# A gated linear recurrence fused with a two-layer MLP: a fourth pair of blocks with two tokens per partition, v reordered by matmul, and a recalibrated instruction order

## The chip, the cores and the metric

The kernel runs on one core of one Trainium2 chip. The metric is the device time of one execution in microseconds (us), lower is better. Of the kernel before there are 11 timed runs, and one execution was recorded by the hardware profiler.

## The reference

For 4 batches, 8 heads, 768 tokens and 48 features per head, a state of 48 x 48 is carried along the tokens, and its output feeds an MLP whose activation is a scaled square of relu plus a bias:

```python
for t in range(S):
    state = alpha[:, :, t, :, None] * state + np.einsum('bhd,bhe->bhde', k[:, :, t], v[:, :, t])
    y[:, :, t] = np.einsum('bhd,bhde->bhe', q[:, :, t], state)
x = y.transpose(0, 2, 1, 3).reshape(3072, 384)
h = x @ w_in                       # 384 -> 2048
r = np.maximum(h, 0.0)
g = s * (r * r) + b
out = g @ w_out                    # 2048 -> 384
```

All inputs and the output are float32; the kernel multiplies in bf16.

## The kernel before

**Blocks.** The 3072 tokens are cut into 24 blocks of 128 (six per batch). Inside a block the recurrence becomes matrix products: the logarithms of alpha are summed along the tokens by a matmul with a triangle of ones (`cum`), exponentials of these sums and of their negatives scale q and k (`qb`, `kb`), scaled q and k are transposed (`T`), their product (`A`, L587) is masked to the triangle (`st_mask`, L597) and multiplied with v (`st_y`, L622); what earlier blocks left comes in through the state (L614), which is updated from k and v (`KV`, `t1`, `snew`). The block's y leaves PSUM (`yevac`), is transposed (`yT`) and lies in `xd` as the MLP's input.

**Two layouts.** The first NPM = 3 pairs of blocks (blocks 0 to 5) are loaded with two neighbouring tokens per partition, so that a contiguous piece of an input is 96 floats (384 bytes); each of the four inputs of a pair is one DMA (L339). From block 6 on, blocks are loaded one by one, one token per partition, with pieces of 48 floats (192 bytes, L346). Four slots per input hold two blocks each (NIN = 4), so a load for block n waits until block n - 8 has been read. In a pair, the tokens of its two blocks lie in the two halves of the partitions, and v must be reordered for `st_y`: it is cast by POOL (L476), half is copied in place (`st_vkeep`, on DVE for pairs 0 and 1, by DMA on SP's queue for pair 2), and half crosses the partitions by DMA (`st_vcross`, from ACT's queue for pairs 0 and 1, from SP's for pair 2). Scaled q and k are transposed by PE up to block 11 and by DMA transposes from SP's queue from block 12 (`st1_Tdma`, L695); y is transposed by PE up to block 13 and by DMA from block 14 (L735).

**The MLP.** Blocks are gathered in groups (GROUPS: 1, 1, 2, 1, 1, 2, 4, 2, 2, 4, 4 blocks). The first product is cut in 96 units of 512 output columns (`mm1`, L755): 12 matmuls of 128 columns, 6 of 256 or 3 of 512, by the size of the group. ACT takes the relu (L764, two buffers `r`), DVE squares it into `gt` (L776). The second product goes in 96 quads (`mm2`, L783), four matmuls of 384 columns each, four quads to a block. The first 12 outputs are scaled by ACT (`oscale`, L815) and get their bias on POOL (`obias`, L824), the later 12 take both steps on DVE (`oevac`, L792). SP stores them. The bias row is made from column sums of w_out (seven large additions on DVE, one float32 matmul, L402).

**Weights.** w_in comes in four quarters by DMAs from POOL's queue, which cast to bf16 on the way (L360). A small copy on POOL (`touch`, L357) ahead of each quarter makes it wait for an input: AFTER = q1, q1, k1, v1. Unit j of a group of one block needs quarter j. w_out comes in four float32 parts by SP's queue and is cast in halves by ACT (L374).

**What sets the order.** A planner in the kernel (`Schedule`) takes a list of operations, each with an engine, an assumed duration, a due time, its tiles and its PSUM bank; it plays the engines forward and always starts the ready operation with the earliest due time. The instructions are emitted in the order of the planned starts, and each engine works its own list in that order. Due times are `want(n)` for block n (from LEAD, UNIT and SHRINK) plus an offset per kind of operation (OFF), and the unit's or quad's number times UNIT for the MLP. SP's loads follow the list LOADS where it names them, then the order of the blocks; moves and stores on SP come as soon as they are ready. Up to 36 us of planned time, small matmuls on zeros (`warm`, L1021) fill planned gaps on PE.

**PSUM.** A of any block goes to one tile of two banks (`a_ps`); the other six banks are handed out by the planner. At most three hold units of the first product.

Of the kernel before, what the change touches and what calls it, by code (L numbers as in the profile page):

```python
# [13 lines left out]
GROUPS = [1, 1, 2, 1, 1, 2, 4, 2, 2, 4, 4]  # L14
LEAD = 28.0
UNIT = 1.7
RING = 8
NPM = 3
NIN = 4
# [5 lines left out]
N_DVE_K = 2  # L25
N_ACT_V = 0
N_ACT_T = 1
N_ACT_X = 2
AFTER = ['q1', 'q1', 'k1', 'v1']
N_POOL_BIAS = 12  # L30
NOUT = 4
TLAT = 3.0
OFF = {'ln': -0.1, 'v': 0.2, 'vk': 0.3, 'vx': 3.95, 'cum': 2.1, 'bl': 1.05, 'ble': 0.2, 'exp': -1.9, 'qb': 0.6, 'kb': 0.1, 'T': -1.6, 'Tc': 0.4, 'KV': 2.65, 't1': 1.2, 'sn': 0.4, 'A': 0.5, 'mask': -1.6, 'y': 1.0, 'ye': 1.2, 'yT': 0.75, 'yTc': 2.9}

LOADS = 'a0 k0 q0 v0 a1 q1 k1 v1 a2 k2 v2 a3 k4 k3 v4 q2 o0 o1 v3 q3 a4 o2 q4 o3 a5 q5 v5 a6 k5 q6 k6 v6 a7 q7 k7 v7 v8 q8 a9 q9 k9 v9 k8 a8 a10 q10 v10 k10'


class Schedule:
# [6 lines left out]
    HOP = 0.3  # L45
    BACKLOG = 4.0

    warm_mates = "cPyYb"
# [11 lines left out]
    def op(self, eng, dur, prio, fn, *args, r=(), w=(), lat=0.1, dma=None, take=(), drop=None):  # L60
        me = len(self.ops)
        deps = set()
# [16 lines left out]
    def run(self):  # L79
# [10 lines left out]
        for i, o in enumerate(self.ops):  # L90
            free.setdefault(o[0], 0.7)
            ready.setdefault(o[0], [])
            if not left[i]:
                ready[o[0]].append((0.0, i))
# [19 lines left out]
        def may(b, i, at):  # L114
            return b or at > self.warm_until or self.ops[i][8][0][0] in self.warm_mates
# [10 lines left out]
        while todo:  # L126
# [13 lines left out]
            if dma is None:  # L140
                free[e] = end[i] = t + dur
            elif eng == "ACT":
# [3 lines left out]
            elif eng == "POOL":  # L146
                free[e] = t + dur
                at = max(t + 1.3, soft)
# [33 lines left out]
    def emit(self, warm):  # L182
        begin = self.run()
        last = 1.0
        for i in sorted(range(len(self.ops)), key=lambda i: (begin[i], i)):
            if self.ops[i][0] == "PE":
                if begin[i] < self.warm_until:
                    warm(max(0.0, begin[i] - last - 0.5))
                last = self.end[i]
            self.ops[i][3](*self.ops[i][4])  # L190
# [15 lines left out]
def kernel(  # L206
# [34 lines left out]

    def p_of(n):
# [33 lines left out]

    la_sb = many("la", 2, [128, 2, H, 64], BF16, zero=nc.vector)
# [16 lines left out]
    zeros_bf = sb.tile([128, 64], BF16, name="zeros_bf")  # L294
    nc.vector.memset(zeros_bf, 0.0)  # L295
    ident_bf = sb.tile([128, 128], BF16, name="ident_bf")
    make_identity(nc, ident_bf)
    for x in range(2):
# [72 lines left out]
    def cast_w_out(i, e):  # L371
        dst = w_out_bf[:, 4 * i + 2 * e : 4 * i + 2 * e + 2]
        src = wst[i][:, 768 * e : 768 * (e + 1)].rearrange("a (j m) -> a j m", j=2)
        nc.scalar.activation(out=dst, in_=src, func=AF.Copy)  # L374
# [96 lines left out]
    def st_vcast(m):  # L471
        dst = vb_sb[m % 2].rearrange("a t (h d) -> a t h d", h=H)
        if m < N_ACT_V:
            nc.scalar.activation(out=dst, in_=tokens(pair_in(v_in, m)), func=AF.Copy)
        else:
            nc.gpsimd.tensor_copy(out=dst, in_=tokens(pair_in(v_in, m)))  # L476

    def st_vkeep(m):
        for e in range(2):
            rows = slice(R * e, R * e + R)  # L480
            if m < N_DVE_K:
                nc.vector.tensor_copy(out=vt_sb[m % 2][rows, e], in_=vb_sb[m % 2][rows, e])
            else:
                nc.sync.dma_start(out=vt_sb[m % 2][rows, e], in_=vb_sb[m % 2][rows, e])

    def st_vcross(m):
        lo, hi = slice(0, R), slice(R, 2 * R)
        eng = nc.scalar if m < N_ACT_X else nc.sync
        eng.dma_start(out=vt_sb[m % 2][hi, 0], in_=vb_sb[m % 2][lo, 1])
        eng.dma_start(out=vt_sb[m % 2][lo, 1], in_=vb_sb[m % 2][hi, 0])  # L490
# [87 lines left out]

    def st_A(n):
# [4 lines left out]
        for p in range(NP):  # L584
            for e in range(2):
                rows = slice(64 * e, 64 * e + 64)
                nc.tensor.matmul(  # L587
                    out=a_ps[:, e, p, :],
# [6 lines left out]
    def st_mask(n):  # L595
        mk = mask.rearrange("a t j -> a (t j)") if n < 2 * NPM else mask_one
        nc.vector.tensor_tensor(  # L597
            out=am_sb[n % 2].rearrange("a e p t -> a (e p) t"),
            in0=a_ps.rearrange("a e p t -> a (e p) t"),
            in1=mk.unsqueeze(1).to_broadcast([128, H, 128]),  # L600
# [130 lines left out]
    def st_yTcopy(n):  # L731
        nc.scalar.activation(out=x_of(n), in_=yt_of(n), func=AF.Copy)
# [93 lines left out]
    sched = Schedule(len(banks), {"c": 2, "T": 2, "P": 2, "y": 2, "Y": 2, "h": 3, "o": 2, "b": 1}, WARM_UNTIL)  # L826
# [11 lines left out]
    for rank, item in enumerate(loads):  # L838
        x, i = item[0], int(item[1:])
        ranks[x, i] = rank - 1000  # L840
        if x == "o":
            op("SP", 0.5, rank - 1000, load_w_out, i, w=[("wst", i)], lat=1.2, dma=2.2)
            for e in range(2):
                op("ACT", 0.78, -400, cast_w_out, i, e, r=[("wst", i)], w=[("wob", i, e)])
            more = "colsum" in sched.writer
            op("DVE", 0.88, COLP, colsum_part, i, more, r=[("wst", i)],
               w=["colpart" if more else "colsum"])
            if more:
                op("DVE", 0.88, COLP, colsum_add, r=["colpart"], w=["colsum"])

    def pair_loads(m):
        for x, (src, dst) in tensors.items():
            op("SP", 0.75, ranks[x, m], load_pair, m, src, dst,
               w=[(x, m % NIN, 0), (x, m % NIN, 1)], lat=1.2, dma=1.45)

    def block_loads(n):
        for x, (src, dst) in tensors.items():
            op("SP", 0.6, ranks[x, n], load_block, n, src, dst, w=[(x, n // 2 % NIN, n % 2)],
               lat=1.2, dma=1.03)

    for m in range(NPM):
# [3 lines left out]
    for i in range(4):  # L865
        x = AFTER[i][0], int(AFTER[i][1:])
        op("POOL", 0.06, -3000 + i, touch, x, r=[(x[0], x[1], 0) if x[1] < NPM else (x[0], x[1] // 2 % NIN, x[1] % 2)], w=[("touch", i)])
        op("POOL", 0.9, -3000 + i, load_w_in, i, r=[("touch", i)], w=[("wib", i)], lat=1.2, dma=2.3)
    op("POOL", 0.8, COLP - 5, bias_mul, w=["bones"])
# [6 lines left out]
    def pair_ops(pm):  # L876
# [3 lines left out]
        t = want(c0)  # L880

# [6 lines left out]
        op("ACT", 0.85, t + OFF["ln"], st_ln, pm, r=io("a"), w=la)  # L888
# [171 lines left out]
```

## Time and profile before

| | us |
|---|---|
| median of 11 runs | 195.68 |
| lowest and highest | 193.46, 198.08 |
| profiled execution, own time | 194.58 |
| its span (first to last instruction) | 192.8 |
| PE busy | 174.4 |
| DVE busy | 132.0 |
| ACT busy | 114.8 |
| POOL busy | 56.9 |

The profiled execution is 1.1 us shorter than the median. A busy engine is one with an instruction in flight; matmuls overlap, so PE's busy time is not its work. PE's work is better read from the starts of neighbouring groups of matmuls where PE is dense. "The chain that ended last" follows the last instruction back to whatever released it; a row of it gives the start, the length and the engine with line, or a DMA by its tiles. The table of stages gives for each stretch the busy time of each engine, the granted TensorE clock (1.00 is full), the mean busy share of the 16 DMA engines and what they moved. In this program, "relu" rows of ACT and "square" rows of DVE are L764 and L776, and "unit 3" means the unit that is the first to read the last quarter of w_in.

### The profile page before, as it was taken

What the parts mean: (1) busy time and instruction counts of PE and PEld (TensorE: products, weight loads), DVE (VectorE), ACT (ScalarE), POOL (GpSimd) and SP (SyncE); (2) the same over time, 40 slices, a digit from 0 to 9 for tenths busy, and PEclk for the clock granted to TensorE, in tenths of its full rate; (3) what the DMA queues carried; (4) which work ended last, traced back from release to release, by engine and by line L of the source; (5) the groups of instructions that cost most, each with busy time, mean ns of one, the idle gap of its engine ahead of it and who ended that gap; (6) DMA issues with size and microseconds to landing.
All of it is one profiled execution on the core that took longest, in us unless ns stands there. A gap on an engine that the chain in (4) does not pass through costs nothing.

```text
span 192.8 us, 4764 instructions
## 1 busy us (share of the span) xinstructions
PE 174.4 (90%) x1847; PEld 118.9 (62%) x1847; DVE 132.0 (68%) x237; ACT 114.8 (60%) x246; POOL 56.9 (30%) x102
## 2 busy tenths in 40 slices
PE   0948948899998999999999999997999999999992
PEld 0836837767876877875655677774655555454561
DVE  6185835899999989979859777774486663354321
ACT  2443336899877848796787677854538561566000
POOL 7549221031729049163425107115141000000000
PEclk9996699999999999999999999999999999999999
DMA  4999999989997899999999989869997311210122
GB/s 109 262 294 232 205 230 383 336 143 190 203 201 169 205 179 198 191 170 220 206 168 203 197 167 205 211 137 190 145 237 209 94 34 20 82 46 2 41 82 83
DMA packets 112407, 33.15 MB, mean 172 GB/s; under 512 B 105216, under 2 KB 112384, under 8 KB 112384
## 3 DMA queue, kind: packets, MB, share of 16 engines
q1 hardware_dynamic: 110176, 31.07, 73.9%
q0 software_dynamic: 1600, 1.57, 4.9%
q8 instruction: 14, 0.23, 0.5%
q10 hardware_dynamic: 608, 0.20, 0.4%
q14 instruction: 9, 0.07, 0.1%
HBM read 25.17 MB, written 4.72 MB: 155 GB/s over the span
## 4 chain that ended last, share of the span: by engine, by line
PE 74%; DMA 12%; SPq 4%; ACT 3%; POOL 2%; DVE 1%; issue 1%; POOLq 0%
PE bank L783 31%; PE bank L755 29%; DMA w_in_bf<-in_moe_w_in_dram 6%; SPq L339 3%; PE a_ps L587 3%; DMA q_in<-in_q_dram 3%; PE bank L622 2%; PE bank L614 2%; DMA a_in<-in_alpha_dram 2%; DMA v_in<-in_v_dram 2%; PE bank L638 2%; PE bank L703 1%; PE bank L682 1%; PE bank L721 1%; POOL w_in_bf L360 1%
## 5 line engine op out<-in xcount | busy, mean ns | idle before, releaser
L755 PE MATMUL bank<-xd,w_in_bf 128*128 128x128 bf16 (+2 forms) x528 | 73.5, 282 | 3.8 <-DMA w_in_bf<-in_moe_w_in_dram 3.8
L764 ACT ACTIVATE r<-bank 128x512 bf16<-128x512 f32 x96 | 56.1, 601 | 27.0 <-PE bank L755 21.2
L783 PE MATMUL bank<-w_out_bf,gt 128*128 128x384 bf16 x384 | 71.9, 326 | 0.0
L755 PEld LDWEIGHTS <-w_in_bf 128*128 128x128 bf16 x528 | 42.2, 98 | 20.9 <-DMA w_in_bf<-in_moe_w_in_dram 4.3
L776 DVE TENSOR_TENSOR gt<-r 128x512 bf16<-128x512 bf16 x96 | 43.1, 469 | 16.9 <-ACT r L764 16.6
L783 PEld LDWEIGHTS <-gt 128*128 128x128 bf16 x384 | 35.4, 97 | 22.2
L572 POOL TENSOR_TENSOR s_st<-t,blast 64x192 bf16<-64x192 bf16 x32 | 19.0, 595 | 26.7 <-DVE t L565 17.4
L597 DVE TENSOR_TENSOR am<-a_ps,mask_one 128x1024 bf16<-128x1024 f32 x18 | 22.0, 1222 | 6.9 <-PE a_ps L587 6.8
L665 POOL CAST vb<-v_in 128x384 bf16<-128x384 f32 x18 | 12.6, 703 | 40.5 <-DMA v_in<-in_v_dram 36.6
L792 DVE SCALAR_TENSOR_TENSOR o_sb<-bank,s_col,bias_w 128x384 f32<-128x384 f32 x12 | 7.4, 617 | 13.3 <-PE bank L783 12.4
L824 POOL TENSOR_TENSOR o_sb<-o_sb,bias_w 128x384 f32<-128x384 f32 x12 | 12.7, 1060 | 11.4 <-ACT o_sb L815 6.8
L716 ACT ACTIVATE yn<-bank 128x384 bf16<-128x384 f32 x24 | 11.8, 492 | 6.1 <-PE bank L622 5.7
L631 ACT ACTIVATE la<-a_in 128x384 bf16<-128x384 f32 x18 | 9.4, 528 | 9.5 <-DMA a_in<-in_alpha_dram 9.4
L1021 PE MATMUL bank<-zeros_bf 128*64 128x64 bf16 x105 | 6.1, 226 | 7.5 <-DVE zeros_bf L295 4.5
L671 DVE TENSOR_TENSOR qk<-k_in,binv 128x384 bf16<-128x384 f32 x18 | 12.4, 688 | 0.2 <-DMA k_in<-in_k_dram 0.2
L653 ACT ACTIVATE b_s<-bank 128x384 f32<-128x384 f32 x18 | 8.8, 490 | 6.1 <-PE bank L643 5.9
L671 DVE TENSOR_TENSOR qk<-q_in,b_s 128x384 bf16<-128x384 f32 x18 | 10.6, 591 | 2.1 <-ACT b_s L653 1.9
L565 DVE TENSOR_TENSOR t<-bank,s_st 128x384 bf16<-128x384 f32 x16 | 8.8, 551 | 4.7 <-PE bank L703 2.1
L587 PE MATMUL a_ps<-qkT 64*128 64x128 bf16 x192 | 10.0, 225 | 1.0 <-DVE qkT L689 0.9
L597 DVE TENSOR_TENSOR am<-a_ps,mask 128x1024 bf16<-128x1024 f32 x6 | 7.3, 1218 | 4.5 <-PE a_ps L587 4.5
L1021 PEld LDWEIGHTS <-zeros_bf 128*64 128x64 bf16 x105 | 5.5, 141 | 7.9 <-DVE zeros_bf L295 4.5
L587 PEld LDWEIGHTS <-qkT 64*128 64x128 bf16 x192 | 5.8, 97 | 5.8 <-issue 3.9
(75 smaller groups left out, 174.1 us busy)
## 6 DMA issues: line engine op xcount, KB each, us to landing
a_in<-in_alpha_dram SPq DMA_DIRECT2D x18, 192.0 KB, 3.8
q_in<-in_q_dram SPq DMA_DIRECT2D x18, 192.0 KB, 3.9
k_in<-in_k_dram SPq DMA_DIRECT2D x18, 192.0 KB, 4.0
v_in<-in_v_dram SPq DMA_DIRECT2D x18, 192.0 KB, 4.1
out_dram<-o_sb SPq DMA_DIRECT2D x18, 192.0 KB, 2.0
wst<-in_moe_w_out_dram SPq DMA_DIRECT2D x4, 768.0 KB, 10.4
w_in_bf<-in_moe_w_in_dram POOLq DMA_DIRECT2D x4, 384.0 KB, 11.2
a_in<-in_alpha_dram SPq DMA_DIRECT2D x3, 384.0 KB, 5.9
```

The costliest lines, as they stand in the source:

```text
L572: nc.gpsimd.tensor_tensor(out=s_sb[n % 4][rows, :, cols], in0=t1_sb[n % 2][rows, :, cols], in1=blast(n)[rows].unsqueeze(2).to_broadcast([6 ...
L587: nc.tensor.matmul(out=a_ps[:, e, p, :], lhsT=T[rows, 1, p], rhs=T[rows, 0, p], start=True, stop=True,)
L597: nc.vector.tensor_tensor(out=am_sb[n % 2].rearrange("a e p t -> a (e p) t"), in0=a_ps.rearrange("a e p t -> a (e p) t"), in1=mk.unsqueeze ...
L665: nc.gpsimd.tensor_copy(out=vb_sb[n // 2 % 2][:, n % 2], in_=block_in(v_in, n).rearrange("a h d -> a (h d)"),)
L671: nc.vector.tensor_tensor(out=qk1_of(n)[:, x, :, 0:D], in0=block_in((q_in, k_in)[x], n), in1=(b_sb, binv_sb)[x][n // 2 % 2][:, n % 2], op= ...
L716: nc.scalar.activation(out=yn_sb[n // 2 % 2][:, n % 2], in_=y_of(n), func=AF.Copy)
L755: nc.tensor.matmul(out=hp[:, i * n : (i + 1) * n], lhsT=w_in_bf[:, kk, 128 * j : 128 * (j + 1)], rhs=xd_sb[g % 3][:, kk, 0:n], start=(kk = ...
L764: nc.scalar.activation(out=r_sb[w % 2], in_=bank("h", w), func=AF.Relu)
L776: nc.vector.tensor_tensor(out=dst, in0=r, in1=r, op=ALU.mult)
L783: nc.tensor.matmul(out=op[:, 0:d_model], lhsT=gt_sb[:, slot, j, :], rhs=w_out_bf[:, j, :], start=(j == 0), stop=(j == NJ - 1),)
L824: nc.gpsimd.tensor_tensor(out=o_sb, in0=o_sb, in1=bias_w, op=ALU.add)
L1021: nc.tensor.matmul(out=banks[0][0:64, 448:512], lhsT=zeros_bf[:, 0:64], rhs=zeros_bf, start=True, stop=True,)
```

## The change

- NPM goes from 3 to 4: blocks 6 and 7 become pair 3, so eight blocks have two tokens per partition. All four slots are now loaded as pairs first.
- v of a pair is cast by ACT. For pairs 0 and 1 it is reordered by PE (`st_V`): a selection matrix `sel_bf` (made by POOL at the start) picks the rows, two matmuls of 384 columns for each block, and ACT copies the result out of PSUM (`st_Vcopy`). For pairs 2 and 3 four DMAs on SP's queue do it (`st_Vdma`), after ACT's cast.
- q and k of pair 3 are transposed by two DMA transposes on SP's queue (`st_Tdma`) instead of by PE.
- For the odd block of a pair, A goes to two banks of the planner's six instead of `a_ps`, and the mask works on each half separately.
- Groups of four blocks become groups of two. LEAD goes from 28 to 24.
- The offsets per kind of operation are replaced by a table KIND, and each block and each group gets an offset of its own (BLOCK). The planner's durations are new, and it reckons with DVE operations that slow down beside POOL. LOADS names all loads in a new order, mixing blocks: k of block 16 stands fifth in the list, though each load still waits for its slot.
- w_in's quarters now wait for q1, q1, q1 and k2, and q1 is the seventh load (it was the sixth).
- One half of a part of w_out is cast by POOL; two copies of y into `xd` (blocks 4 and 9) move from ACT to DVE; four outputs (blocks 8 to 11) move from ACT and POOL to DVE.
- The filler matmuls are 128 x 256 instead of 64 x 64, and `zeros_bf` is cleared first.

The core of the diff (the new tables KIND, BLOCK and LOADS are shortened):

```diff
-GROUPS = [1, 1, 2, 1, 1, 2, 4, 2, 2, 4, 4]
-LEAD = 28.0
+GROUPS = [1, 1, 2, 1, 1, 2, 2, 2, 2, 2, 2, 2, 2, 2]
+LEAD = 24.0
-NPM = 3
+NPM = 4
+N_PAIR_T = 3
+N_PE_V = 2
+POOL_CASTS = [3]
+POOL_V = [5]
+DVE_VC = [4, 7]
+DVE_YC = [4, 9]
-AFTER = ['q1', 'q1', 'k1', 'v1']
-N_POOL_BIAS = 12
+AFTER = ['q1', 'q1', 'q1', 'k2']
+N_POOL_BIAS = 8
-LOADS = 'a0 k0 q0 v0 a1 q1 k1 v1 a2 k2 v2 a3 k4 k3 v4 q2 o0 o1 v3 q3 a4 o2 q4 o3 a5 q5 v5 a6 k5 q6 k6 v6 a7 q7 k7 v7 v8 q8 a9 q9 k9 v9 k8 a8 a10 q10 v10 k10'
+LOADS = 'a0 a1 v0 k0 k16 q0 v1 q1 k1 a2 k2 q8 a16 a3 q2 o0 o1 o2 v2 k8 o3 v23 k3 q12 k12 a11 q3 q15 q19 k14 a8 v3 v8 q16 a9 q9 ...'
...
+    def a_of(n, e):
+        if split(n):
+            return bank("A", 2 * n + e).rearrange("a (p t) -> a p t", p=NP)
+        return a_ps[:, e]
...
+    def st_V(m, c):
+        for t in range(2):
+            nc.tensor.matmul(
+                out=bank("V", 2 * m + c)[:, 0 : H * D],
+                lhsT=sel_bf[:, c, t, :],
+                rhs=vb_sb[m % 2][:, t],
+                start=(t == 0),
+                stop=(t == 1),
+            )
+
+    def st_Vcopy(m, c):
+        dst, src = vt_sb[m % 2][:, c], bank("V", 2 * m + c)[:, 0 : H * D]
+        if 2 * m + c in DVE_VC:
+            nc.vector.tensor_copy(out=dst, in_=src)
+        else:
+            nc.scalar.activation(out=dst, in_=src, func=AF.Copy)
+
+    def st_Vdma(m):
+        vb, vt = vb_sb[m % 2], vt_sb[m % 2]
+        for c in range(2):
+            for t in range(2):
+                nc.sync.dma_start(
+                    out=vt[R * t : R * t + R, c], in_=vb[R * c : R * c + R, t]
+                )
...
+    def split(n):
+        return n < 2 * NPM and n % 2 == 1
...
+        prio += KIND.get(fn.__name__, 0.0)
+        if blk is not None:
+            prio += BLOCK[blk]
```

## The prediction

> **What bounds the kernel now.** I read the page's first part, then the chain that ended last, in order of time, then the table of stages.
>
> ```profile
> span 192.8 us, 4764 instructions
> PE 174.4 (90%) x1847; PEld 118.9 (62%) x1847; DVE 132.0 (68%) x237; ACT 114.8 (60%) x246; POOL 56.9 (30%) x102
> ```
>
> PE is the bound on average, but the 90% hides a slow start. From the chain:
>
> ```profile
> 13.69 0.76 POOL w_in_bf L360
> ...
> 18.35 11.96 DMA w_in_bf<-in_moe_w_in_dram
> 30.36 2.18 PE bank L755 x36
> ...
> 58.76 1.35 DVE qk L671
> 60.11 0.61 DVE qkT L689
> 60.77 0.40 PE a_ps L587 x8
> ...
> 115.51 3.31 DMA a_in<-in_alpha_dram
> 118.85 0.53 ACT la L631
> ...
> 178.13 11.06 PE bank L783 x68
> 189.22 0.62 DVE o_sb L792
> ```
>
> Columns: start, length, what. The fourth quarter of w_in lands at 30.36, and only then does the first product (L755) run freely. The last 68 matmuls take 11.06 us, 0.163 each, so a group of four (128x384) or one unit of the first product (512 columns) is 0.65: this is PE at its best. PE ends at 189.2; the last eviction, store and end make 3.6 more (span 192.8), and 1.8 lie outside it (own time 194.58).
>
> The stages, cut at the fourth quarter (30.36) and at unit 24 of the first product (73.03):
>
> ```profile
> 30.36:73.03 42.67, 41.00 (x571) 32.33 (x572) 38.73 (x66) 34.07 (x76) 15.04 (x18) 1.00 0.95 218
> 73.03:189.00 115.97, 114.54 (x1006) 71.44 (x1003) 75.11 (x137) 68.87 (x149) 26.64 (x40) 1.00 0.71 144
> ```
>
> Columns: length, busy PE, PEld, DVE, ACT, POOL, granted clock, DMA share, GB/s. In the first DVE is busy for 38.7 of 42.7: it bounds this stage as much as PE, as the chain at 58.76 says. The second is PE's.
>
> **PE's own work.** From starts of neighbouring pieces where PE is dense: unit or group 0.65; A 0.33; y 0.25, with the state 0.42; KV 0.18; yT 0.17; cum of a block 0.27; T 0.45; of a pair cum 0.65 and bl 0.2, KV 0.40 (0.22 for pair 2's one chunk); bias 0.7. Multiplied with the built order, the kernel before has 161.7 us of PE work, 8.9 of it ahead of unit 3, the first to read w_in's fourth quarter. The rest is 152.8: 30.36 + 152.8 = 183.2, against a measured 189.0. So PE lost 5.8 after the gate: unit 24 started 42.7 after unit 3 where the sum says 39.2 (3.5 lost beside DVE), and 2.3 later, at the loads for blocks 18 to 20 (the chain at 115.51).
>
> **The Trainium skill.** (1) DMA: Bandwidth & Descriptors, Specifications, puts full rate at pieces from 512 B up. The trace agrees in direction: 288 GB/s in 10 to 16 us, where pieces are 384 B, 192 in 80 to 110, mostly 192 B, at DMA shares of 1.05 and 1.06. (2) Same page, Queues, rings and completion order: each DMA engine takes turns between queues. So w_in, on POOL's queue, shares with SP's; its quarters gate units at 25.1, 27.7 and 30.36, 2.65 apart, while loads continue. (3) TensorE: Matmul & The Clock Gate, Part 1: a window of about 3.4 us without enough work halves the clock. The trace shows 0.50 from 16 to 22 us after a thin stretch (PE busy 0.54 of 2 us at 12 to 14). (4) SBUF — State Buffer, Who interferes with whom: a DVE instruction with two SBUF inputs blocks against GpSimd's reads. The k products average 688 ns where undisturbed ones take 550.
>
> **The change, part by part.**
>
> *PE.* v for pairs 0 and 1: 8 matmuls of 384 columns, 8 x 0.163 = +1.3. Pair 3 in place of blocks 6 and 7: two T go to DMA (-0.9), cum 0.85 for 0.54 (+0.3), KV 0.40 for 0.36. Sum 162.5 (+0.8). Groups of two for the last fours: 0.65 per 512 columns at every width, so nothing. Filler matmuls fall from 105 to 28, wider ones; they stand only ahead of unit 0, where PE waits anyway, so I price them, and any clock gained there, at nothing. If they overfilled, bound 28 x 0.21 = 5.9, a wait for w_in covers it.
>
> *The gate.* q1, whose landing starts w_in's issue, is now the seventh load (sixth before). Between a0's use at 5.29 and q1's at 13.26 loads land (13.26 - 5.29)/5 = 1.59 apart, so the gate goes 1.6 later: 32.0. The fourth quarter now waits for k2, the tenth load (v1 was the eighth); with shares as before it lands near 21.5, ahead of the third quarter's end (29.3), so it stays in line. Bounds: 30.4, if q8's wait on SP thins SP's traffic, to 34.5. But PE now does 14.3 ahead of unit 3, not 8.9 (V, cum of pairs 2 and 3, one T of pair 2, all y of pair 1, unit 5). Remaining: 148.1, not 152.8.
>
> *DVE and ACT.* Up to unit 24, by row means (square 0.45, masks 1.22, products 0.55 to 0.62, copies 0.69, sums of w_out 0.95): from the square of unit 3 to that of 24, DVE had 46.9 and now has 34.5; ACT 43.5, now 32.6; PE 39.2, now 35.7. LEAD 24 and more attention before the gate do this. v's copies on DVE go (4 x 0.249); ACT takes four casts (128x768; 0.84, from the row of la) and four v copies (0.49), nearly all ahead of the gate. One w_out cast goes to POOL (bounds 0.85 and 1.1, beside other work). Split masks: half-size 0.61 to 1.22, I take 0.68, four blocks, +0.6. Two xd copies on DVE: 0.25 to 0.69, I take 0.35. Four outputs move from ACT and POOL to DVE, 4 x 0.617 = 2.5 after unit 24, where DVE is busy 75 of 116: covered. With DVE and ACT just under PE I keep 1.5 of the 3.5 lost.
>
> *SP's queue.* Four loads of 384 KB replace eight of 192: 1.57 MB at 288 for 192 GB/s, 5.5 for 8.2 us, -2.7. v of pairs 2 and 3 is eight transfers of 48 KB; such moves from SP took 8.6 to land. Pair 3's wait for ACT's cast; behind them stand finished stores (3, 7, 11) and the loads for blocks 15 and 16. ACT reaches that cast near 53, the move lands near 63, and y of block 7 stands near 64 (45.2 of PE work done): 1 us of cover, beyond which PE waits. The two transposes of pair 3 (3.7 to land) have more. Stores of blocks 6 and 7 become two each, two issues of 0.6.
>
> Loads now go out by planned use, not by block, so k17, k20 and k22 have 25.0, 27.5 and 29.8 MB ahead of them. By the GB/s slices, 21.5 MB had moved at 100 us before; less 2.7, at 97.3. At 195 GB/s (the mean of 84 to 110 is about that at a full share) they follow at 115.6, 128.4 and 140.1, and 3 us later in use (before's a20 and a22 were used at 118.85 and 133.5 where the same count gives 115.9 and 130.5). My sum puts units 48, 56 and 64 at 112.8, 125.4 and 139.1, and PE can run 5 units (3 banks, 2 buffers of r: 3.3 us) before a DVE that waits for k stops it. 118.6 - 116.1 = 2.5; 131.4 - 128.7 = 2.7; 143.1 - 142.4 = 0.7. They overlap, so I take the largest, 2.7, in place of the 2.3 lost late.
>
> **The sum.** Unit 24 starts at 32.0 + 35.7 + 1.5 = 69.2 (73.0 before); PE ends at 69.2 + 112.4 + 2.7 = 184.3 (189.2 before); + 3.6 + 1.8 = 189.7 as own time, against 194.58: -4.9, -2.5%. On the median of the runs, 195.68 (1.1 above the profiled one): 190.8.
>
> **Rivals.**
>
> *A, the loads become the bound (slower).* If the holds on SP's queue, first at pair 3's v, leave the DMA engines short of work and eat the 2.7 saved, and the pace is 165 GB/s (that of 132 to 140, at share 1.10), k22 lands at 100 + 8.3/0.165 + 3 = 153.6 where PE can stand 142.4: a loss of 11.2 in place of 2.7. Own time 198.2, median 199.3. It is slower from a loss of about 8.5 on. For: DMA share is 1.05 to 1.14 from 84 to 108, so nothing is in hand; the new order loads k16 and q16 ahead of q10. Against: from 108 to 132 the share is 0.77 to 0.95, so some is, later.
>
> *B, the gate comes later.* SP's w_out loads (large pieces) go out among w_in's quarters, and k2 lands late: gate at 36.5, losses as forecast: median 195.3, no change. For: the quarters wait for more loads. Against: the fourth took 11.96 from issue to landing, so it was queued anyway.
>
> *C, DVE costs nothing and the gate stays at 30.4:* PE ends at 30.4 + 148.1 + 1.5 = 180.0, median 186.5.
>
> **Chances.** Forecast 0.57, own range 188 to 194; A 0.19; B 0.13; C 0.11. A measurement of this kernel tells about 0.5%, 1 us, from no change. A reaches from 196 to 202, B from 193.5 to 197. Faster than 194.7: 0.57 + 0.11 + 0.05 of B = 0.73; slower than 196.7: 0.17 of A and 0.01 of B = 0.18; between: 0.09. The range, 186.7 to 198, leaves out the lower half of C and the upper half of A.
>
> **What would show it.** Right: first unit reading w_in's fourth quarter near 32 with y of pair 1 done ahead of it; unit 24 near 69; DVE idle for some us between 32 and 69; PE's end near 184; DVE waits of 2 to 3 us for k near 118 and 131. A would show as waits of twice that and PE's end past 190; B as a gate after 35; a late v as PE waiting for vt between 45 and 66. I am wrong if PE stays dense and the end doesn't move: then my PE prices are off.

## The result and the profile after

The changed kernel takes 198.12 us, the median of 12 runs (196.39 to 202.54); the kernel before, run beside it, 195.58, the median of 47 (192.63 to 198.08). The ratio is 1.017, 95% interval 1.013 to 1.021: 1.3 to 2.1% slower, where the forecast was 190.8. Here and below, a ratio leaves out runs that took over 1.5% longer than the fastest run of the same kernel, two of these twelve. The profiled execution of the changed kernel, the fastest of the twelve, took 196.39 for a span of 194.6, against 194.58 for 192.8 before. In the lines below, line numbers are those of the changed kernel: L806 and L834 are the two products of the MLP, L679 is the logarithm of a block, L458 that of a pair, L783 the copy of y into `xd`.

```profile
span 194.6 us, 4895 instructions
PE 179.1 (92%) x1916; PEld 133.6 (69%) x1916; DVE 131.9 (68%) x241; ACT 116.2 (60%) x245; POOL 51.3 (26%) x99
```

PE is busier than before and the kernel is slower all the same. A busy share doesn't tell waiting from work at half clock; the chain that ended last does. Its columns are start, length, what.

```profile
13.50 10.09 DMA a_in<-in_alpha_dram
24.88 1.01 PE bank L552 x8
26.86 2.67 PE bank L806 x24
...
33.16 1.34 PE bank L806 x24
...
71.62 3.85 DMA a_in<-in_alpha_dram
...
77.93 4.55 PE bank L806 x24
...
89.03 1.33 PE bank L806 x12
...
117.96 4.69 DMA a_in<-in_alpha_dram
...
129.83 4.38 DMA k_in<-in_k_dram
...
144.75 3.05 DMA v_in<-in_v_dram
...
184.54 6.51 PE bank L834 x40
```

w_in, which stood in the chain before, is gone from it. In its place are five loads: a of pair 3 (a3) at the start, a of block 10 (a10) at 71.62, and three late ones. Counting units along the planned order gives the positions: the row at 33.16 holds units 5 and 3, so unit 3 starts at 33.8; the row at 89.03 begins with unit 32. Unit 24 is in PE's order of time (the bracket is the wait ahead of a row):

```profile
70.25 2.12 PE L806 MATMUL bank<-xd,w_in_bf 128*128 128x256 bf16 x18
72.21 0.33 PE L769 MATMUL bank<-ident_bf,yn 128*128 128x128 bf16 x3
76.06 0.48 PE L686 MATMUL bank<-la,U_one 128*128 128x384 bf16 x1 [3.53 <-ACT la L679]
76.34 0.29 PE L691 MATMUL bank<-ones_col,la 128*128 128x1 bf16 x4
76.48 1.44 PE L834 MATMUL bank<-w_out_bf,gt 128*128 128x384 bf16 x4
77.72 4.75 PE L806 MATMUL bank<-xd,w_in_bf 128*128 128x256 bf16 x24
```

PE stood for 3.53 us behind a logarithm, and the 24 matmuls at the end of these rows took 4.75 us instead of 2.6. ACT's order of time names the loads behind both stalls:

```profile
23.61 0.84 ACT L458 ACTIVATE la<-a_in 128x768 bf16<-128x768 f32 x1 [2.92 <-DMA a_in<-in_alpha_dram]
24.36 0.85 ACT L783 ACTIVATE xd<-bank 128x384 bf16<-128x384 bf16 x2
...
75.49 0.52 ACT L679 ACTIVATE la<-a_in 128x384 bf16<-128x384 f32 x1 [4.56 <-DMA a_in<-in_alpha_dram]
```

At the start, pair 3's logarithm waits for a3 and stands ahead of the two copies of y that unit 0 needs. Later block 10's logarithm waits for a10, with the relus of unit 24 and later units behind it. Why a10 was late stands in SP's queue, in order of time:

```profile
51.62 1.59 SPq L373 DMA_DIRECT2D k_in<-in_k_dram  x1
53.31 3.02 SPq L568 DMA_TRANSPOSE qkT<-qk  x2
56.45 2.46 SPq L529 DMA_DIRECT2D vt<-vb  x4
59.01 4.84 SPq L858 DMA_DIRECT2D out_dram<-o_sb  x6
63.94 0.54 SPq L373 DMA_DIRECT2D k_in<-in_k_dram  x1
...
71.62 0.79 SPq L373 DMA_DIRECT2D a_in<-in_alpha_dram  x1
```

From 53.3 to 63.9 no load goes out: pair 3's two transposes, its four moves of v and six stores of half blocks stand in a row. Then seven loads (k16, a16, q15, q16, v15, k11, q14) go ahead of a10. All but k11 are used later than a10; for k11, which went out at 70.09, DVE waited 4.24 us, until 73.35. The stages show what this did to the DMA engines; first the changed kernel, then the kernel before (columns as before: busy times, granted clock, DMA share, GB/s).

```profile
50.00:70.00 20.00, 20.00 (x291) 15.34 (x289) 17.07 (x29) 14.04 (x31) 8.52 (x10) 1.00 0.77 163
70.00:110.00 40.00, 36.47 (x372) 27.67 (x371) 26.54 (x50) 26.02 (x61) 10.11 (x17) 0.91 1.01 192
110.00:150.00 40.00, 39.38 (x441) 28.98 (x439) 32.09 (x56) 24.14 (x58) 9.17 (x16) 1.00 0.88 187
60.00:66.00 6.00, 6.00 (x96) 4.86 (x95) 5.24 (x10) 3.33 (x9) 0.86 (x2) 1.00 0.52 119
0.00:50.00 50.00, 42.17 (x464) 31.79 (x465) 34.36 (x65) 34.12 (x66) 20.31 (x51) 0.93 1.02 250
0.00:70.00 70.00, 62.17 (x753) 47.13 (x753) 51.43 (x93) 48.15 (x97) 28.82 (x61) 0.95 0.94 225
```

```profile
50.00:70.00 20.00, 19.12 (x271) 15.22 (x269) 18.72 (x35) 13.91 (x34) 9.32 (x11) 1.00 0.91 191
70.00:110.00 40.00, 40.00 (x432) 26.49 (x431) 34.19 (x59) 32.23 (x76) 17.47 (x25) 1.00 1.04 194
60.00:66.00 6.00, 5.23 (x86) 4.48 (x87) 6.00 (x13) 4.90 (x14) 2.65 (x4) 1.00 0.89 210
0.00:50.00 50.00, 37.51 (x533) 29.99 (x534) 34.53 (x62) 29.47 (x58) 19.14 (x50) 0.93 0.99 236
0.00:70.00 70.00, 56.63 (x802) 45.21 (x803) 53.25 (x96) 43.38 (x91) 28.46 (x60) 0.95 0.97 223
```

Between 50 and 70 us the DMA engines were busy for 0.77 of the time in place of 0.91, and moved 28 GB/s x 20 us = 0.56 MB less, about three loads. PE didn't notice then (20.00 of 20.00); it paid in the next stage, 36.47 of 40, part of it at half clock. From 70 to 110 us the engines are full in both kernels (1.01 and 1.04), so nothing makes the gap good there.

The last two rows of each table put this gap in its place. To 50 us the changed kernel had moved 250 GB/s x 50 us = 12.5 MB, the kernel before 11.8. That lead of 0.7 MB is 2.8 us at the same 250 GB/s, about what the prediction expected to save on SP's queue; how much of it the larger pieces gave was not separated. To 70 us the two had moved about the same, 15.75 and 15.6 MB, and some 0.5 of the 15.75 are pair 3's two transposes (2 x 128 x 1024 values of two bytes). Counted by the loads that have landed, in units of 192 KB (one input of one block), the changed kernel had 36 at 50 us and 46 at 70, the kernel before 33 and 49. So a lead of three had become a lag of three by 70 us, while PE was 2.8 us ahead.

**Where the time went**, by the prediction's own sum: unit 3 at 33.8 (forecast 32.0), unit 24 at 70.25 (69.2), PE's end at 191.05 (184.3). So up to unit 24 the forecast was 1.1 us short, and after it PE took 120.8 us for 112.4 of work: 8.4 lost, where 2.7 were forecast. Of the 8.4, 6.5 lie between unit 24 and unit 32 (89.03 - 70.25, for 12.3 of work by the same prices), and 1.9 after it.

### The profile page after: what moved, and what is told of

Same layout as the page of the kernel before. It is cut to its first block, busy times and chain, and to the rows that moved or that the text cites. A ratio compares the mean times of both kernels' runs of the same rounds, so it can differ in the third digit from the quotient of the medians.

```text
span 194.6 us, 4895 instructions
## 1 busy us (share of the span) xinstructions
PE 179.1 (92%) x1916; PEld 133.6 (69%) x1916; DVE 131.9 (68%) x241; ACT 116.2 (60%) x245; POOL 51.3 (26%) x99
## 4 chain that ended last, share of the span: by engine, by line
PE 59%; SPq 15%; DMA 13%; DVE 4%; ACT 3%; issue 3%; POOL 0%; ACTq 0%; DVEq 0%
PE bank L806 26%; PE bank L834 23%; DMA a_in<-in_alpha_dram 10%; SPq L366 6%; SPq L373 6%; DMA k_in<-in_k_dram 2%; PE a_ps L631 2%; DVE am L645 2%; DMA v_in<-in_v_dram 2%; PE bank L670 1%; SPq L786 1%; DVE gt L827 1%; ACT r L815 1%; PE bank L686 1%; PE bank L662 1%
## 5 line engine op out<-in xcount | busy, mean ns | idle before, releaser
L806 PE MATMUL bank<-xd,w_in_bf 128*128 128x256 bf16 (+1 forms) x672 | 75.8, 265 | 0.0
L834 PE MATMUL bank<-w_out_bf,gt 128*128 128x384 bf16 x384 | 73.5, 328 | 0.0
L806 PEld LDWEIGHTS <-w_in_bf 128*128 128x128 bf16 x672 | 58.6, 101 | 10.1 <-issue 0.5
L834 PEld LDWEIGHTS <-gt 128*128 128x128 bf16 x384 | 35.1, 98 | 18.1 <-issue 0.3
L645 DVE TENSOR_TENSOR am<-a_ps,mask_one 128x1024 bf16<-128x1024 f32 x16 | 19.5, 1220 | 2.7 <-PE a_ps L631 2.6
L713 POOL CAST vb<-v_in 128x384 bf16<-128x384 f32 x16 | 8.9, 556 | 34.3 <-DMA v_in<-in_v_dram 18.3
L719 DVE TENSOR_TENSOR qk<-k_in,binv 128x384 bf16<-128x384 f32 x16 | 10.5, 659 | 8.4 <-DMA k_in<-in_k_dram 6.7
L764 ACT ACTIVATE yn<-bank 128x384 bf16<-128x384 f32 x24 | 11.8, 494 | 6.9 <-PE bank L670 6.6
L843 DVE SCALAR_TENSOR_TENSOR o_sb<-bank,s_col,bias_w 128x384 f32<-128x384 f32 x16 | 9.8, 615 | 8.0 <-PE bank L834 8.0
L679 ACT ACTIVATE la<-a_in 128x384 bf16<-128x384 f32 x16 | 8.4, 534 | 6.8 <-DMA a_in<-in_alpha_dram 6.8
L875 POOL TENSOR_TENSOR o_sb<-o_sb,bias_w 128x384 f32<-128x384 f32 x8 | 8.7, 1101 | 10.3 <-ACT o_sb L866 7.0
L670 PEld LDWEIGHTS <-am 128*128 128x128 bf16 x192 | 7.4, 97 | 1.9 <-issue 1.3
L686 PE MATMUL bank<-la,U_one 128*128 128x384 bf16 x16 | 5.3, 336 | 3.5 <-ACT la L679 3.5
L701 ACT ACTIVATE binv<-bank 128x384 f32<-128x384 f32 x16 | 8.1, 506 | 0.0
```

What stands on the lines that cost most here:

```text
L645: nc.vector.tensor_tensor(out=dst, in0=src, in1=mk.unsqueeze(1).to_broadcast([128, dst.shape[1], 128]), op=ALU.mult,)
L701: nc.scalar.activation(out=(binv_sb if inv else b_sb)[n // 2 % 2][:, n % 2].rearrange("a h d -> a (h d)"), in_=cb[:, 0 : H * D], func=AF.E ...
L719: nc.vector.tensor_tensor(out=qk1_of(n)[:, x, :, 0:D], in0=block_in((q_in, k_in)[x], n), in1=(b_sb, binv_sb)[x][n // 2 % 2][:, n % 2], op= ...
L764: nc.scalar.activation(out=yn_sb[n // 2 % 2][:, n % 2], in_=y_of(n), func=AF.Copy)
L806: nc.tensor.matmul(out=hp[:, i * n : (i + 1) * n], lhsT=w_in_bf[:, kk, 128 * j : 128 * (j + 1)], rhs=xd_sb[g % 3][:, kk, 0:n], start=(kk = ...
L834: nc.tensor.matmul(out=op[:, 0:d_model], lhsT=gt_sb[:, slot, j, :], rhs=w_out_bf[:, j, :], start=(j == 0), stop=(j == NJ - 1),)
```

## Experiments

All ratios are to the kernel before on the same chip; the changed kernel's is 1.017 (1.013 to 1.021). The expectations in us suppose the kernel before at 195.6; on the chips of these runs it took 192.8 to 193.2, so it is the ratios that compare, and times in us from two profiles compare only roughly. The changed kernel as it is was not run again on these chips, so its 1.017 is taken over from the first measurement; two edits (filled gap, order of first readers) came out at the same 1.017 and 1.0175. "Order kept" means that the planned order of emission is taken over as it is and single entries are moved; each pair (a, b) of MOVES puts a ahead of b:

```python
for a, b in MOVES:
    i, j = names.index(a), names.index(b)
    seq.remove(i)
    seq.insert(seq.index(j), i)
```

My first theory was the two stalls: take away each wait, and the time comes back. The rival was that the loads as a whole set the pace.

### a10 and k11 earlier

```diff
+MOVES = [('load_block:10,a', 'load_block:16,k'), ('load_block:11,k', 'load_block:16,k')]
```

> The changed kernel with every engine's order kept, only that the loads a10 and k11 go out on SP's queue ahead of the load k16 (that is, right behind the stores of blocks 1, 2 and 3, near 64 us, in place of 71.6 and 70.1). Theory (the time went into ACT's wait for a10 and into the halved TensorE clock behind it): the 3.5 us in which PE stood at 72.5 and the 3 us lost at clock 0.50 up to 82 both go; unit 24 to unit 32 take about 13 us in place of 19; median near 192 (191 to 194), below both kernels. Rival 1 (the loads as a whole are the bound; whatever is put first, another is late): some other load stalls PE by as much, median 196 to 198. Rival 2 (only the wait counts, the clock would have fallen anyway): median 194.5 to 195.

Measured: 1.025 (1.020 to 1.030), not faster at all. (The stores ahead of these loads are those of blocks 0, 1 and 2.) The wait went to another load. ACT's order of time in this run:

```profile
70.61 0.51 ACT L696 ACTIVATE la<-a_in 128x384 bf16<-128x384 f32 x1
...
80.92 0.52 ACT L696 ACTIVATE la<-a_in 128x384 bf16<-128x384 f32 x1 [5.80 <-DMA a_in<-in_alpha_dram]
```

Block 10's logarithm (here L696) no longer waits; block 12's, ten us later, waits 5.80. The theory that these two loads alone were late fell; rival 1 held.

### Pair 3's logarithm behind the copies

```diff
+MOVES = [('st_ln:3', 'relu:0')]
```

> The changed kernel with every order kept, only that ACT takes the logarithm of pair 3 (which waits for a3) behind the two copies of y of blocks 0 and 1 instead of ahead of them. Theory (a3 at ACT set the start, w_in's quarters are the next gate): the copies run near 21 instead of 24.4, unit 0 then waits for w_in's first quarter, unit 3 starts near 30.5 in place of 33.0; median 1 to 3 us below the changed kernel, about 196. Rival 1 (w_in's quarters gate the units as in the kernel before, and a3's wait was in their shadow): within 0.5 us of the changed kernel. Rival 2 (all of the wait and the slow clock behind it go): 5 to 6 us less, about 192.5.

Measured: 1.015 (1.011 to 1.019), within the noise of the changed kernel. The start did improve: the 21st relu began at 59.3 us in place of 61.8. But PE's wait for the later logarithms grew from 3.5 to 6.3 us: PE came earlier to the logarithm of block 10, whose load did not come earlier, and got past it at 75.84 in place of 76.06. The waits of PE, longest first (total, times, longest):

```profile
PE bank L703 <- ACT la L696: 6.3, 2, 5.7
...
PE bank L823 <- DMA w_in_bf<-in_moe_w_in_dram: 1.4, 2, 1.0
```

### The gap filled with matmuls

```diff
+            if self.name(i) == "st_yT:8":
+                j = next(j for j in range(len(self.ops)) if self.name(j) == "mm1:26")
+                for _ in range(5):
+                    self.ops[j][3](*self.ops[j][4])
```

> The changed kernel with every wait left in place, and 30 more matmuls on PE in the gap at 72.5: the product of unit 26 is written five more times, 3.25 us by the dense price, behind the transposes of y of block 8 and ahead of the wait for a10's logarithm. Theory (the idle PE lost its clock, and that cost about 3 us of the loss): the clock stays near 1.00 from 76 to 82, the 24 matmuls of L806 behind the gap take 2.6 us in place of 4.6, median 2 to 3 us below the changed kernel, about 195.5. Rival (the clock fell for another reason, or what was lost at half clock was hidden by later waits): the same as the changed kernel, about 198, or slower by the added work.

Measured: 1.017 (1.012 to 1.021), no change. The clock did what was expected. The stage of 76 to 82 us, changed kernel and then this run:

```profile
76.00:82.00 6.00, 5.93 (x31) 3.89 (x31) 3.00 (x6) 4.95 (x13) 1.75 (x3) 0.52 0.91 190
```

```profile
76.00:82.00 6.00, 6.00 (x63) 4.64 (x61) 3.85 (x9) 5.33 (x15) 1.69 (x3) 1.00 1.01 202
```

At full clock PE did twice the matmuls in these 6 us, but the timed runs show no gain; by their intervals about 1 us could hide there. The profiled execution was 2 us shorter than the changed kernel's, which says little: on this chip the kernel before is 2.7 us faster, too. The reading that fits is that the time at half clock falls in a stretch in which PE would have waited for loads anyway. The two rows agree with the Trainium skill (TensorE: Matmul & The Clock Gate, Part 1), by which about 3.4 us without enough work halve the clock: 3.5 us of idling gave 0.52, a filled gap 1.00.

### Both edits of order

```diff
+MOVES = [('load_block:10,a', 'load_block:16,k'), ('load_block:11,k', 'load_block:16,k'), ('st_ln:3', 'relu:0')]
```

> The first two edits together: a10 and k11 ahead of k16, and pair 3's logarithm behind the two copies. Theory: the two stalls lie in different stages and add up: median near 190 (188.5 to 192), some 5 us below the kernel before. Rival (one pace of loads bounds both: work that starts earlier meets loads that are not there yet): no better than the loads' edit alone, 192 or more.

Measured: 1.014 (1.010 to 1.017). The gains don't add up; PE still waits up to 5.6 us for a block's logarithm. So far the rival, one pace of loads, had every point.

### All later loads in the order of their first readers

```diff
+EARLY = 27
...
+        loads = [x for x, i in enumerate(seq) if names[i].startswith(("load_p", "load_b"))][EARLY:]
+        left = [seq[x] for x in loads]
+        use = {i: min(begin[u] for u in range(len(seq)) if i in self.ops[u][5]) for i in left}
+        for x in loads:
+            i = min((i for i in left if self.ops[i][5] <= set(seq[:x])), key=use.get)
+            left.remove(i)
+            seq[x] = i
```

> The changed kernel with every engine's order kept, and SP's queue too except for which load stands in which place: from the 28th load on, each place takes the load whose first reader comes first. Moving a10 and k11 alone had only handed the wait on to a12, six places further back. Theory (the loads stand in the wrong order: k16, a16, q15, q16, v15, q14, v12 and v14 go out before a10, a12 and a13, 1.6 MB or 8 us at 200 GB/s): the stall between 72 and 81 goes, unit 32 starts near 83 in place of 89, and some of it is lost again later since the loads as a whole end no earlier: ratio to the kernel before 0.985 to 1.00. Rival (the pace of all loads together bounds, in whatever order): the wait turns up at another load, ratio 1.01 to 1.02.

Measured: 1.0175 (1.012 to 1.023). The stall at 72 did go: the 33rd relu began at 84.1 in place of 89.9. Then DVE stood from 90.2 to 95.0 us:

```profile
95.04 0.56 DVE L744 TENSOR_TENSOR qk<-q_in,b_s 128x384 bf16<-128x384 f32 x1 [4.83 <-DMA qkT<-qk]
```

By the order this is block 16's product, which must not overwrite `qk` until block 12's DMA transpose, itself behind loads in SP's queue, has read it. The gain of 5.7 us at the 33rd relu was down to 0.4 at the 49th (118.8 in place of 119.2); this wait behind the same queue is the largest of DVE's on the way. The ratio is the rival's.

> The same order of loads, and pair 3's logarithm behind the two copies of y on ACT. Theory (order): the 2.3 us gained at the start reach the end in part: ratio 0.975 to 0.995. Rival (pace of all loads): as the edit before, 1.01 to 1.015.

With pair 3's logarithm moved as well: 1.010 (1.007 to 1.014). This is at most slightly better than the changed kernel (the intervals just overlap) and short of the 0.995 that the theory of order wanted.

### Fewer bytes

In the changed kernel and in the kernel before, the loads of q for blocks 8 to 23 are left out (these blocks read older data):

```diff
     def load_block(n, src, dst):
+        if src is q and n >= 8:
+            return
```

> The changed kernel without the loads of q for blocks 8 to 23 (these blocks read what an earlier load left in the same buffer): 16 transfers and 3.1 MB less, all else in place; its time shows what the kernel costs with a quarter of the later loads taken away. Theory (the load stream paces PE from 70 to 148 us): the stall at 72 to 81 and the late ones go, PE's end is near its work of 162.5 plus the 20.5 us that it is behind at unit 24, so 183 to 185 in place of 191; ratio to the kernel before 0.965 to 0.98. Rival (order on ACT and DVE, or TensorE's clock, not the loads): 1.005 to 1.02.

> The kernel before without the loads of q for blocks 8 to 23, in the same way. Theory (there too the loads set the late part, DVE the part up to unit 24): PE falls behind by 2 us less late: ratio 0.985 to 0.99, so less than the changed kernel gains. Rival 1 (it is as much bound by loads as the changed kernel): 0.97. Rival 2 (not bound by loads at all): 1.00.

Measured: the changed kernel 0.968 (0.961 to 0.974), 5% less than with these loads, as expected; the kernel before 0.996 (0.994 to 0.998), 0.4% less, nearer to "not bound by loads" than was expected. After 40 us PE has not one wait in the list of the changed kernel's run. Its stages:

```profile
50.00:70.00 20.00, 19.99 (x289) 15.68 (x286) 16.77 (x27) 13.27 (x30) 8.70 (x11) 1.00 0.79 169
70.00:110.00 40.00, 40.00 (x442) 30.38 (x440) 31.95 (x59) 28.66 (x70) 13.08 (x22) 1.00 1.02 185
110.00:150.00 40.00, 40.00 (x442) 30.23 (x441) 32.65 (x60) 25.41 (x56) 7.99 (x14) 1.00 0.61 136
```

PE is busy for 40.00 of 40.00 twice, at clock 1.00. From the 21st to the 93rd relu it took 111.8 us where the changed kernel took 118.9. This shows the bound: with a quarter of the later loads gone, the changed kernel no longer waits, so between 70 and 150 us its loads set its pace; those of the kernel before hardly do. The share of 1.02 in the second row is a warning: full DMA engines alone don't mean that PE waits. And with loads out of the way the change is worth 0.968 / 0.996 = 0.972 (0.965 to 0.978, worked out from the two intervals), a gain of 2.8% where 2.5% was forecast.

> The changed kernel with the loads of q and k for blocks 8 to 23 cut to four of eight heads (the rest of the buffer keeps what an earlier load left): as many transfers as before, but 3.1 MB less, just as without q. It tells bytes from issues. Theory (DMA engines are full, share 0.94 to 1.0 from 70 to 150 us, so bytes count): ratio 0.965 to 0.98, as without q. Rival (SP's issue of one load after the other, 0.6 to 0.9 us each, paces the stream): 1.005 to 1.02.

```diff
+        hs = H // 2 if src is q or src is k else H
         nc.sync.dma_start(
-            out=block_in(dst, n),
-            in_=src[b, :, c * C : (c + 1) * C, :].rearrange("h s d -> s h d"),
+            out=block_in(dst, n)[:, 0:hs],
+            in_=src[b, 0:hs, c * C : (c + 1) * C, :].rearrange("h s d -> s h d"),
```

Measured: 0.972 (0.967 to 0.976), the same as without q. As many transfers stand on the queue, the same number of bytes less, and PE again has no wait in the list after 40 us. So the bytes count here (or the pieces of 192 bytes, which were halved with them), not the number of loads on the queue.

### SP's queue opened, and pair 3's transfers left out

Opened: two loads between pair 3's transposes and its moves of v, the stores of blocks 0, 1 and 2 apart and later. Nothing is left out.

```diff
+MOVES = [('st_Vdma:3', 'load_block:15,q'), ('ostore:3', 'load_block:15,v'),
+         ('ostore:7', 'load_block:12,v'), ('ostore:11', 'load_block:10,k')]
```

> Only the opening of SP's queue, in the changed kernel as it is (loads in its own order, logarithm where it was). Theory (the hole): a10 goes out 2 to 3 us earlier, the wait at 72 falls below 2 us; ratio 1.00 to 1.01 against 1.017. Rival (order of the loads, not the hole): 1.015 to 1.02.

Measured: 1.006 (1.0035 to 1.008), 1.1% below the changed kernel, by moving four entries of one queue. a10 went out at 68.5 in place of 71.6, PE's wait for its logarithm fell from 3.5 to 0.7 us, and the share of the first stage rose from 0.77 to 0.86. The edit brought a wait of its own: the later store of block 0 kept ACT from writing into the same output buffer for 3.03 us, and PE stood 2.28 us behind ACT, all that is missing of the 20 us in the stage's row. So the 1.1% is what is left after this wait. The stage and the row of ACT:

```profile
50.00:70.00 20.00, 17.72 (x266) 13.88 (x264) 14.98 (x27) 12.41 (x28) 7.53 (x9) 1.00 0.86 181
```

```profile
68.21 0.58 ACT L883 ACTIVATE o_sb<-bank,s_col 128x384 f32<-128x384 f32 x1 [3.03 <-DMA out_dram<-o_sb]
```

> Loads in order of use, pair 3's logarithm behind the two copies of y, and now SP's queue opened between 53 and 64 us, where it issued two transposes, four moves of v and six stores in a row and no load, and where the DMA engines were busy for 0.45 to 0.7 only: two loads stand between pair 3's transposes and its moves of v, and the stores of blocks 0, 1 and 2 stand apart behind later loads. Theory (the loads' stream is the bound, and this hole is the part of it that the change made): the DMA share of 50 to 70 us rises from 0.75 to 0.85 or more, 2 to 3 us come out at the end: ratio to the kernel before 0.99 to 1.00, against 1.010 without the opening. Rival (the stream is full from 70 to 150 anyway and what it lost earlier doesn't matter): 1.005 to 1.015.

With all three edits (queue opened, loads by first reader, logarithm moved): 1.004 (0.9995 to 1.008). The fourteen runs spread from 192.1 to 198.1 us, and their median, 195.4, is 1.011 of the kernel before; the 1.004, which comes from the five fastest, is weak. Against 1.006 with the queue opened alone, no further gain from the loads' order and the start is shown. (The share of 0.45 to 0.7 that the expectation gives for 53 to 64 us is not what the trace shows: it is 0.98 from 53 to 56 us and 0.30 from 58 to 62.)

> The changed kernel with pair 3's two transposes and four moves of v on SP's queue left out (blocks 6 and 7 read what pair 1 left in these buffers), all else in place. Theory (these six transfers hold SP's queue for 5.5 us and fill the DMA engines for some 4 us of poor traffic): the loads behind them go out 5.5 us earlier, PE's wait at 72 goes, ratio 0.985 to 1.00. Rival (the stream from 70 us on is the bound whatever went before): 1.01 to 1.017.

```diff
     def st_Vdma(m):
+        if m == 3:
+            return
...
     def st_Tdma(m):
+        return
```

Measured: 0.983 (0.978 to 0.988), 3.4% below the changed kernel and faster than before, with this work left out: blocks 6 and 7 read what pair 1 left in the same buffers. SP's queue in order of time:

```profile
51.13 0.66 SPq L373 DMA_DIRECT2D k_in<-in_k_dram  x1
53.39 4.89 SPq L861 DMA_DIRECT2D out_dram<-o_sb  x6
...
66.17 0.80 SPq L373 DMA_DIRECT2D a_in<-in_alpha_dram  x1
```

a10 goes out 5.4 us earlier, what the six transfers had held the queue for. The theory held: its range ended at 0.985. In the profiled execution not all of the gain comes after the start. There a3 was ready by 19.7 us in place of 23.6, with nothing changed ahead of it, and unit 0 came 5 us earlier. From the 21st to the 93rd relu this execution took 116.3 us; the changed kernel took 118.9, and the profiles with the other loads' orders, the filled gap and the opened queue (logarithm in place) 117.5 to 119.4. So 1 to 3 us come after the start here, and the early start reaches the end, which it did not in the second experiment. The six timed runs took 188.6 to 192.6, the profiled one 190.7, so the 3.4% doesn't hang on this one execution; how it splits in the others isn't shown. Of the 3.4%, opening the queue gives 1.1 with no work left out; what the DMA time of the transfers and the waits of pair 3 give is not separated here. Which of the two kinds, transposes or moves of v, costs more was not measured, and neither was the new layout with loads in the order of the kernel before.

### No transposes by DMA

Every transpose on PE, in both kernels; the order is planned anew for it. Nothing is left out, PE has 8.0 us more work (7.1 in the kernel before, which has no N_PAIR_T and takes the last two edits).

```diff
-N_PAIR_T = 3
+N_PAIR_T = 4
...
-N_PE_T = 12
-N_PE_Y = 14
+N_PE_T = 24
+N_PE_Y = 24
```

> The changed kernel with every transpose that went by DMA (pair 3's q and k, q and k of blocks 12 to 23, y of blocks 14 to 23) done by PE and copied by DVE or ACT, its order made anew for it; v of pairs 2 and 3 still by DMA. PE's work rises by 8.0 us to 170.5, the DMA engines and SP's queue lose 24 transfers. Theory (the stream of loads is what held the changed kernel): no wait of several us for a load from 70 us on; PE's end near 170.5 + 20 = 190.5, the same as with 8 us less work, ratio 1.00 to 1.015. Rival (work on PE, DVE and ACT bounds the changed kernel): all of the 8 us come on top: 1.05 or more.

> The kernel before with the same edit (q and k of blocks 12 to 23, y of blocks 14 to 23): 7.1 us more work for PE, 22 transfers less. It was bound by PE and DVE and hardly by loads, so most of the work comes on top: ratio 1.02 to 1.04; the changed kernel without DMA transposes is then 2 to 3% faster than this one, the gain that was forecast for the change. Rival (the change brings nothing where loads are not in the way): the two within 0.7%.

Measured: 1.0515 (1.045 to 1.058) and 1.039 (1.033 to 1.0445). The first is the rival's number: I missed it. The second lies in its range, but the changed kernel, which should have been 2 to 3% faster than the kernel before with the same edit, is 1.2% slower. The stages of the changed kernel's run show where part of it went:

```profile
70.00:90.00 20.00, 17.70 (x222) 14.54 (x219) 14.35 (x30) 15.07 (x37) 8.16 (x12) 1.00 0.98 202
90.00:110.00 20.00, 18.65 (x230) 15.06 (x229) 15.86 (x29) 13.77 (x32) 4.45 (x6) 1.00 0.93 189
110.00:150.00 40.00, 40.00 (x453) 30.09 (x452) 31.67 (x54) 23.44 (x55) 10.11 (x18) 1.00 0.39 91
```

Apart from pair 3's, the transposes that went from the DMA engines stood after 89 us, so room came after 110 us (share 0.39), too late for a stall at 70 to 100; PE still lost 2.3 and 1.35 us in the first two stages, and 7.1 us at the start, behind a3.

> m1_after with pair 3's logarithm behind the two copies of y on ACT, all else in the same order. With the loads out of the way the 2 us that this gained at the start reach the end: ratio 0.985 to 1.00. Rival (lost again as in the changed kernel): as m1_after.

> m2_start with the loads from the 28th on in the order of their first readers. If the stream keeps ahead of PE, the order doesn't matter: within 0.5% of m2_start. If late loads remain, 0.5 to 1% faster.

Measured: 1.041 (1.036 to 1.046) with pair 3's logarithm moved, and 1.015 (1.009 to 1.021) with the loads in the order of their readers too. Both miss their expectations: the first was to come to 1.00 or less or to gain nothing, the second to gain at most 1%. Here the order of the loads, worth nothing measurable in the changed kernel, is worth 2.5%. The reading that fits: with room in the stream later, what is loaded first is not paid for afterwards. All of PE's waits after 40 us in the last run:

```profile
PE bank L695 <- DMA vt<-vb: 0.7, 2, 0.6
PE bank L794 <- ACT yn L789: 0.4, 1, 0.4
```

It takes as long as the changed kernel with 8 us more for PE to do. It is 2.3% faster than the kernel before without DMA transposes (1.015 / 1.039), though that one had no such repairs. No version that does all the work beat the kernel before; the nearest are those with the queue opened, at 1.004 and 1.006.

## Why the prediction was wrong

**Right: PE's work and prices.** 162.5 us was forecast, with nothing for groups of two. Without q's loads, PE went from the 25th relu at 69.1 to the 93rd at 170.25, 101.1 us, where the sum of the pieces between says 101.4.

**Right in size, wrong in cause: the gate.** Unit 3 came at 33.8, within the bounds of 30.4 to 34.5, but not through w_in: pair 3's logarithm, waiting for a3 ahead of the copies of y, held PE for 3.3 us until 24.9 and left it at half clock (24 matmuls in 2.67 us for 1.3). I had put "any clock gained there, at nothing" and never asked what stands ahead of the copies on ACT. So it was luck that the number lay within the bounds. With the logarithm moved, PE waited 1.4 us for w_in instead.

**Right: DVE up to unit 24.** From unit 3 to 24 took 36.45 us for 35.7 of work: 0.7 lost, forecast 1.5. So the relief of DVE and ACT came as forecast. The 2.8% that the runs without q show are the gain of the change as a whole; how much of them is this relief was not separated.

**Right: pair 3's own cover.** No wait of PE for `vt` or `qkT` is in the list of the profile after; v landed in time.

**The step that failed: "They overlap, so I take the largest, 2.7".** The loss after unit 24 measured 8.4. I compared three loads of k for DVE near 116 to 143 us with the stream's pace, and there the size was fair: 1.9 lost after unit 32. I compared none of the loads before them with the point at which PE, now 2.8 us earlier at unit 24, would want it. The prediction names what "stands behind" pair 3's moves, finished stores and loads for blocks 15 and 16, and prices only whether v is late for pair 3; it never prices what these twelve issues, stores among them, do to the loads further back. It carried the 2.7 us saved on larger pieces through to 97 us, as if nothing would spend them. The runs show that these issues were 10.6 us without a load, that the lead in loads at 50 us was a lag at 70, and that a10 was used only at 75.5 us. An earlier PE doesn't make a full stream earlier: what was gained up to unit 24 (20.2 us of waiting, 70.25 less 50.0 of work, where it had been 24.9, 73.0 less 48.1) was handed back by unit 32, with 6.5 us lost between the two.

**Rival A was the mechanism, in another place.** It said that holds on SP's queue, "first at pair 3's v", leave the engines short of work and eat the 2.7 saved. That is what the share of 0.77 at 50 to 70 us and the lead spent by 70 us show, and opening the queue gives 1.1% back. A put the loss at k22 near 150 us, 11.2 in size; it fell mostly on a10 at 72 and was 8.4, at the edge of A's own 8.5. Its pace of 165 GB/s did not come either: the stage from 70 to 110 us moved 192. So that its 199.3 was only 1.2 off is in part luck. I gave it 0.19 because the share fell to 0.77 to 0.95 after 108 us, but a stream that has room later is no help to a load that is wanted at 72. Rival B and rival C are out: w_in was no gate, and the end came later.

**The range**, 186.7 to 198, was drawn to leave out the upper half of A. The time, 198.1, lies just past its end, near the middle of A.

## What to carry to other kernels

When a change makes the compute engines earlier, list for each in-order engine the next load that it will need and set it against that load's place in the queue, not only the loads at the end; a gain that ran into a full stream was handed back whole here. Price every transfer put on the loading queue twice: for who waits for it, and for the loads behind it. To find whether loads are the bound, take bytes away in both kernels: here it told in one run each what three repaired stalls had not. And when you move a store back to let loads through, look at who needs its buffer next.

## What the runs showed of the hardware

- Half the bytes of q and k in as many transfers gave what leaving out q did, a quarter fewer transfers (0.972 and 0.968): with the DMA engines at a share of 1.0, a load of 192 KB in pieces of 192 bytes costs by its bytes or its pieces, not by being one more load on the queue.
- Issues add up when they stand together: two transposes 3.02 us, four moves of 48 KB 2.46, six stores of 96 KB 4.84, and the DMA engines were down to a share of 0.52 from 60 to 66 us (0.89 before).
- 3.5 us without matmuls gave 0.52 of the clock for the next 6 us; 30 matmuls in the gap kept 1.00. That the time was the same with and without it (1.017 and 1.017) I had not expected.
- The same load, a3, with the same instructions ahead of it, was ready by 19.7 us in one of six profiled executions and at 22.6 to 24.1 in the five others. How long an in-order engine stands behind such a load differs from one execution to the next; one profile shows one case.
